# An attention and feed-forward kernel on one core: pacing of the weight decoder in the last slot of a round, order of the first score block, one load in one transfer, other PSUM banks for the first accumulators

## The chip, the core and the metric

The kernel runs on one core of a Trainium2 chip. The metric is the device time of one execution in microseconds. The kernel before took 1028.57 us in the median of three runs (1028.46 to 1028.59). Its engines are TensorE (matmuls; its weight loads are listed on their own), VectorE, ScalarE, GpSimd and SyncE, called PE, PEld, DVE, ACT, POOL and SP in the profile. SP here only issues transfers.

## What is computed

Sigmoid attention over 8 sequences of 448 positions with 12 heads of 64, then a feed-forward network on the 3584 tokens. Everything is float32.

```python
scores = scale * np.matmul(q, k.transpose(0, 1, 3, 2)) - np.log(S)   # (8, 12, 448, 448), scale 1/8
attn = 1.0 / (1.0 + np.exp(-scores))
attn_out = np.matmul(attn, v)
x = attn_out.transpose(0, 2, 1, 3).reshape(3584, 768)
h = x @ w_in                       # (768, 2048)
out = np.maximum(0.01 * h, h) @ w_out
```

## The kernel before

Float32 products are made of parts: each operand is split into a high part (a copy in the type fp32r, which TensorE multiplies fast) and a low part (the operand less its high part), and a product takes three matmuls: high by high, high by low, low by high.

**Attention** works on 48 pairs of heads (`Pair`, line 476), two pairs, x and y, in each of 24 rounds (line 794). A round has five slots: the scores of x, the scores of y, P·V of x, P·V of y, and an ending with the last keys' scores of the next pair (`last_scores`) and the last values' products (`last_v`). The keys come in blocks of 128 (c = 0, 1, 2), each with a PSUM tile of two banks, from four such tiles, which P·V uses too; the last 64 keys are handled two pairs at a time in the ending. While a round runs, the operands of the next round's pairs (z, w) are made ready: high parts on ScalarE or VectorE, low parts on VectorE, z's in slot 3 and w's in slot 4 (line 807). After P·V, ScalarE copies one half of the result to x (`half`), and after `last_v`, in the first slot of the next round, VectorE adds the other half (`keep`, line 577; `x<-x,pv` in the profile).

**Order.** Every instruction is pinned to program order on its engine. Chores for later slots are put in lists by `later`; `slot` runs the chores of its slot, then the slot's matmuls.

**Decoder.** The weights arrive as 64-bit floats. VectorE decodes them in five steps for each piece (lines 423 to 431), then adds and subtracts blocks for the fast matrix product (`firsts` for w_in, `second` for w_out), and SP stores the blocks to HBM. `prep` is a generator with one step for each `next`. In attention `prepare` (line 449) takes steps from it after each slot's work: a slot earns `PACES[n]` credits, a step costs one, and steps are taken while VectorE's counted queue is under `TIMES[n]` less 0.2. The count is kept by `counted` (line 145): 0.14 us plus columns/960 or columns/1920 for each VectorE instruction. At the end of a slot `TIMES[n]` is taken off the queue. In the feed-forward stage `fill` takes steps in a like manner.

**First feed-forward product** (`First`, line 688): seven products of a fast matrix scheme in two levels of blocks; a `Quad` of accumulators holds px, py and pz. Its PSUM pool `ps_f` has two tiles px and two tiles pz of two banks each; two unused pz tiles are taken first, so that pz has banks 0 to 3 and px banks 4 to 7. The first quad's px lay in banks 4 and 5. **Second product**: the loop over `PRODUCTS`, with operands from HBM. The change doesn't touch it.

**Start.** Pair 0's queries and keys come in four transfers, two issued by ScalarE and two by SP (`load_qk`, line 483), pair 1's in two, one on each. ScalarE then loads its sigmoid table with a small warm-up activation. `split` (line 505) makes pair 0's parts in pieces: ScalarE casts the two query halves, VectorE casts the keys and makes the low parts of keys, first and second query half, in this order. Meanwhile TensorE runs dummy matmuls into a tile `unread` (line 788). The first two score blocks are issued in halves of 224 queries (`scores`, line 516), sorted by this key (m is the part product: 0 high by high, 1 high keys by low queries, 2 low keys by high queries):

```python
todo.append((c, (m > 0 and c + 1, m, cols.start), dict(...)))
```

So both blocks' high products come first (first half of queries of block 0, then of block 1, then the second halves), then the rest of block 0, then the rest of block 1.

Of the kernel before, what the change touches and what calls it, by code (L numbers as in the profile page):

```python
# [17 lines left out]
P = 128  # L18
# [7 lines left out]
ST = 7  # L26
# [4 lines left out]
PACES = 4, 5, 4.2, 2.8, 2  # L31
TIMES = 1.92, 1.92, 2.33, 2.33, 1.66
PRODUCT, LESS, MOST = 1.8, 0.2, 4
WAIT, REST = 9, 3
FFN = 126
ALONE = 100
# [65 lines left out]
def attn_ffn_kernel(ctx: ExitStack, tc: tile.TileContext, qk, v, w_in, w_out, out):  # L102
# [240 lines left out]
    def firsts(u, dec):  # L343
        to = td[u // 2][:, :, u % 2]
        dma(out=to[:, :3], in_=dec[:, 1:])

        b12, b22, b11, b21 = (dec[:, i] for i in range(4))
        sums = block(F32, (4, HW), f"ws0_{u}")
        for place, x, y in ((2, b12, b11), (0, b22, sums[:, 2]), (1, b22, b12), (3, b21, sums[:, 0])):
            sub(sums[:, place], x, y)  # L350
            yield
        dma(out=to[:, 3:], in_=sums)

    def rest():
# [3 lines left out]
    def second(u, k, dec):  # L358


        n = len(BLOCKS)
        size = wide // 2
        e, at = u // 2, u % 2 * size
        both = {side: dec[i].rearrange("p a b -> p (a b)").rearrange("p (n m) -> p n m", n=n) for i, side in enumerate("ds")}

        def of(n, side, at, step):
            x = both[side]
            if step == 0:
                return x[:, at:at + 1].broadcast_to((P, n, size))
            end = at + (n - 1) * step + (1 if step > 0 else -1)  # L370
            return x[:, at:end if end >= 0 else None:step]

        for what, *x in PLAIN.get(k, STEPS):
            if what == "wait":
                yield from rest()
            elif what == "store":
                side, i, n, form = x
                dma(out=t2d[:, form:form + n, e, at:at + size], in_=both[side][:, i:i + n])
            else:
                n, fn, *x = x  # L380
                to, x, y = (of(n, *z) for z in x)
                if fn == "neg":
                    vec_st(out=to, in0=x, scalar=-1.0, in1=y, op0=ALU.mult, op1=ALU.subtract)
                else:
                    (add if fn == "add" else sub)(to, x, y)
                yield

    def prep():

        n = 4
        pieces = [(m, k) for m in range(len(todo)) for k in range(n)]
        raws = []

        def load():
            at = len(raws)
            if at == len(pieces):
                return
            m, k = pieces[at]  # L400
            w, u = todo[m]
            size = 4 * HW // n
            pool = (stage, "stage", 2 * HW, STAGE) if at % 2 and now < ALONE else (pp, "wr", 2 * HW, 3)
            raw = block(I32, (size, 2), f"wr{w}_{u}_{k}", pool)
            dma(out=raw.rearrange("p m t -> p (m t)"), in_=(w_in, w_out)[w][u][:, k * size:(k + 1) * size].bitcast(I32))
            raws.append(raw)

        for _ in range(3):
            load()
        yield  # L410
        for at, (m, k) in enumerate(pieces):
            w, u = todo[m]
            if k == 0 and w == 0:
                dec = block(F32, (4, HW), f"wd{w}_{u}")
            elif k == 0:
                both = [block(F32, (4, HW), f"wd{w}_{i}") for i in range(2)] if u == 0 else both[::-1]
                dec = both[0]
            raw = raws[at]
            size = 4 * HW // n
            low, high = raw[:, :, 0], raw[:, :, 1]  # L420
            tf = dec.rearrange("p b m -> p (b m)")[:, k * size:(k + 1) * size]
            t = tf.bitcast(I32)
            vec_s(out=t, in0=high, scalar1=0x7FFFFFFF, scalar2=None, op0=ALU.bitwise_and)
            yield
            vec_s(out=tf, in0=tf, scalar1=W_LEAST, scalar2=W_MOST, op0=ALU.max, op1=ALU.min)
            yield
            vec_s(out=t, in0=t, scalar1=5, scalar2=2, op0=ALU.logical_shift_left, op1=ALU.logical_shift_right)
            yield
            vec_st(out=t, in0=high, scalar=-0x40000000, in1=t, op0=ALU.bitwise_and, op1=ALU.bitwise_or)
            yield  # L430
            vec_st(out=t, in0=low, scalar=29, in1=t, op0=ALU.logical_shift_right, op1=ALU.bitwise_or)
            yield
            while len(raws) < min(at + 1 + (5 if now < ALONE else 3), len(pieces)):
                load()
            if now < ALONE:
                yield
            if w == 1:
                yield from second(u, k, both)
            elif k == n - 1:
                yield from firsts(u, dec)  # L440
            if k == n - 1:
                prepared.add((w, u))
                if w == 0:
                    yield from rest()

    preps = prep()
    credit = 0.0

    def prepare(pace, time):
        nonlocal credit, queue  # L450
        credit += pace
        while credit >= 1 and queue < time - LESS:
            next(preps, None)
            credit -= 1
        queue = max(0.0, queue - time)

# [19 lines left out]
    class Pair:  # L476
# [6 lines left out]
        def load_qk(self):  # L483
            self.raw = raws.tile([P, LAST.stop], F32, tag="qk", name=f"qk_{self.i}")
            middle, end = QUERY + S // 2, LAST.stop
            for queue, cols in {
                    0: ((dma_act, slice(QUERY, middle)), (dma, KEYS[0]), (dma_act, slice(middle, end)), (dma, slice(2 * P, QUERY))),
                    1: ((dma_act, slice(QUERY, end)), (dma, slice(0, QUERY)))}.get(self.i, ((dma, slice(0, end)),)):
                queue(out=self.raw[:, cols], in_=qk[self.i, :, cols])

        def load_v(self):
# [24 lines left out]
        def scores(self, h):  # L516
            todo, acts = [], []
            for c in range(2 * h, min(2 * h + 2, NK - 1)):
                ps = psum("s", f"sc_{self.i}_{c}")

                for cols in HALVES if self.i == h == 0 else (slice(0, S),):
                    for m, (kp, qp) in enumerate(((0, 0), (0, 1), (1, 0))):
                        for j, me in enumerate(heads):
                            todo.append((c, (m > 0 and c + 1, m, cols.start), dict(
                                out=ps[:, j, cols], lhsT=self.parts[me, kp, c * P:c * P + P],
                                rhs=self.parts[me, qp, query(cols)], start=m == 0 and cols.start == 0,
                                stop=m == 2 and cols.stop == S, skip_group_check=True)))
                acts.append((c, ps))
            if self.i == h == 0:
                todo.sort(key=lambda x: x[1])  # L530
            for n, (c, ps) in enumerate(acts):
                for x in todo if self.i == h == 0 and n == 0 else [x for x in todo if x[0] == c and (self.i or h)]:
                    mm(**x[2])
                self.a.append(self.attn(c, ps))
# [153 lines left out]
    class First:  # L688
# [6 lines left out]
        def step(self):  # L695
            t = (self.p + 1) * NU * NOP - len(self.todo)
            u, n, e = self.todo.pop(0)
            advance(t)
            p = self.p
            if n == ORDER[0] and e == 0:  # L700
                self.quad = Quad(psum, st, "st", f"h{p}_{u}", ST, leaky)
                self.c = Results()
            quad, c = self.quad, self.c
            w = w1[t // 2][1].t[:, e]
            acc, first = quad.into(n, e)
            hi, lo = self.ops.hi[n], self.ops.lo[n]
            for kk in range(NB):
                parts_mm(acc, w, slice(kk * P, kk * P + P), hi[:, kk], lo[:, kk], first and kk == 0, kk == NB - 1)
            if e == 0:
                return  # L710
            if u == NU // 2 - 1:
                self.ops.used(n)
            later(1, lambda: self.after(quad, c, u, n), first=True)
# [80 lines left out]
    for r in range(rounds):  # L794
# [15 lines left out]
        for n, work in enumerate(works):  # L810
            go([(ops[0], PLAN_ATTN.get((r, n), ""))], work)
            for t in EARLY.get((r - rounds + 1, n), ()):
                advance(t)
            prepare(PACES[n] * (r > 0), TIMES[n])

    kept, chores[now] = chores[now][0], ([], chores[now][1])
    for fn in kept:
# [4 lines left out]

    st = left.enter_context(tc.tile_pool(name="st", bufs=ST, reuse_waits="tile"))
    tiles(left, "m", "left", MORE)
    psum = banks("ps_f", dict(px=(2, 2), pz=(2, 2)))
    for n in range(2):
        psum("pz", f"first_{n}")
    size = NU * NOP

    def product(q, first, k):  # L830
# [336 lines left out]
```

## Time and profile before

| what | value |
|---|---|
| median of three runs | 1028.57 us |
| profiled execution, its own time | 1029.18 us |
| its span, first to last instruction | 1027.40 us |
| PE busy | 1023.2 us |
| PEld busy | 867.8 us |
| DVE busy | 857.2 us |
| ACT busy | 598.1 us |
| DMA | 301.1 MB, 293 GB/s in the mean |

The profile is one execution recorded by the hardware; times count from its first instruction. "Idle before" is an engine's idle time just ahead of an instruction, with what ended it, inferred from semaphores; "issue" means that nothing in the profile ended it. Where the releaser named had long been done, it was not what was waited for. The attention stage lasts to about 246 us, the first product to about 650, the second to the end.

### The profile page before, as it was taken

What the parts mean: (1) busy time and instruction counts of PE and PEld (TensorE: products, weight loads), DVE (VectorE), ACT (ScalarE), POOL (GpSimd) and SP (SyncE); (2) the same over time, 40 slices, a digit from 0 to 9 for tenths busy, and PEclk for the clock granted to TensorE, in tenths of its full rate; (3) what the DMA queues carried; (4) which work ended last, traced back from release to release, by engine and by line L of the source; (5) the groups of instructions that cost most, each with busy time, mean ns of one, the idle gap of its engine ahead of it and who ended that gap; (6) DMA issues with size and microseconds to landing.
All of it is one profiled execution on the core that took longest, in us unless ns stands there. A gap on an engine that the chain in (4) does not pass through costs nothing.

```text
span 1027.4 us, 16361 instructions
## 1 busy us (share of the span) xinstructions
PE 1023.2 (100%) x6316; PEld 867.8 (84%) x6316; DVE 857.2 (83%) x1015; ACT 598.1 (58%) x634; POOL 0.3 (0%) x5
## 2 busy tenths in 40 slices
PE   9999999999999999999999999999999999999998
PEld 6555555556999999999999999999999999999998
DVE  5889999789998899898975657699988888899883
ACT  7888888887545655555555555565362535444440
POOL 0000000000000000000000000000000000000000
PEclk9999999999999999999999999999999999999999
DMA  8888787989889898989986878997678797767833
GB/s 308 279 298 278 280 281 267 311 292 331 289 312 322 293 298 299 344 317 409 338 296 213 300 283 313 392 408 289 217 282 286 278 416 291 284 221 252 311 113 135
DMA packets 113853, 301.10 MB, mean 293 GB/s; under 512 B 9712, under 2 KB 51696, under 8 KB 113776
## 3 DMA queue, kind: packets, MB, share of 16 engines
q1 hardware_dynamic: 111760, 295.52, 80.5%
q10 hardware_dynamic: 2016, 4.54, 1.2%
q8 instruction: 50, 0.82, 0.3%
q14 instruction: 27, 0.22, 0.1%
HBM read 203.16 MB, written 96.86 MB: 292 GB/s over the span
## 4 chain that ended last, share of the span: by engine, by line
PE 99%; ACT 0%; ACTq 0%; DVE 0%; DVEq 0%; issue 0%
PE px_h L139 22%; PE acc_A L139 18%; PE acc_B L139 18%; PE pv L139 13%; PE pz_h L139 11%; PE sc L139 11%; PE py_h L139 6%; PE acc_one L139 0%; ACTq L139 0%; ACT L139 0%; DVE o L139 0%; ACT qks L139 0%; DVEq L1163 0%; ACT warm L139 0%
## 5 line engine op out<-in xcount | busy, mean ns | idle before, releaser
L139 PE MATMUL px_h<-hi,w 128*128 128x448 f32 x768 | 223.1, 361 | 0.0
L139 PEld LDWEIGHTS px_h<-hi,w 128*128 128x128 f32 x768 | 143.9, 187 | 11.3 <-ACT x L139 0.7
L139 PE MATMUL acc_A<-gh,w 128*128 128x448 f32 x528 | 151.4, 361 | 0.0
L139 DVE TENSOR_TENSOR w<-wx,w 128x768 fp32r<-128x768 f32 x112 | 106.9, 955 | 48.2 <-ACT w L139 48.2
L139 PE MATMUL px_h<-lo,w 128*128 128x448 f32 x384 | 139.4, 363 | 0.0
L139 ACT ACTIVATE s<-sc 128x896 f32<-128x896 f32 x144 | 119.4, 934 | 17.7 <-PE sc L139 17.7
L139 PE MATMUL acc_B<-gh,w 128*128 128x448 f32 x416 | 119.4, 361 | 0.0
L139 PE MATMUL pv<-s,v 64*64 64x448 f32 x1152 | 114.0, 540 | 0.0
L139 PE MATMUL pz_h<-hi,w 128*128 128x448 f32 x384 | 112.7, 361 | 0.0
L139 PEld LDWEIGHTS acc_A<-gh,w 128*128 128x128 f32 x528 | 98.9, 187 | 7.4
L139 PEld LDWEIGHTS sc<-qks 64*128 64x128 f32 x876 | 79.9, 187 | 23.6 <-issue 16.2
L139 ACT CAST w<-wx 128x768 fp32r<-128x768 f32 x112 | 92.0, 834 | 10.8 <-DMA wx<-t 10.8
L139 PE MATMUL sc<-qks 64*128 64x448 f32 (+1 forms) x876 | 95.5, 368 | 0.1
L139 PEld LDWEIGHTS pv<-s,v 64*64 64x64 f32 x1152 | 41.6, 133 | 60.9 <-issue 47.7
L139 DVE TENSOR_TENSOR w<-w 128x1536 fp32r<-128x1536 f32 x52 | 91.1, 1752 | 0.0
L139 ACT ACTIVATE c_h<-c_h 128x896 f32<-128x896 f32 x48 | 45.9, 956 | 74.1 <-DVE c_h L139 74.1
L139 PE MATMUL acc_B<-g,w 128*128 128x448 f32 x328 | 84.8, 362 | 0.0
L139 PEld LDWEIGHTS acc_B<-gh,w 128*128 128x128 f32 x416 | 77.9, 187 | 5.8
L139 ACT CAST w<-w 128x1536 fp32r<-128x1536 f32 x52 | 77.1, 1482 | 0.5 <-DMA w<-t 0.5
L139 PEld LDWEIGHTS pz_h<-hi,w 128*128 128x128 f32 x384 | 71.9, 187 | 5.3
L139 PEld LDWEIGHTS px_h<-lo,w 128*128 128x128 f32 x384 | 72.1, 188 | 3.8
L139 DVE SCALAR_TENSOR_TENSOR wd<-wr,wd 128x384 int32<-128x384 int32 x128 | 71.3, 557 | 3.2
(96 smaller groups left out, 1619.1 us busy)
## 6 DMA issues: line engine op xcount, KB each, us to landing
wx<-t SPq DMA_DIRECT2D x112, 384.0 KB, 5.4
w<-t SPq DMA_DIRECT2D x52, 768.0 KB, 4.3
g<-g SPq DMA_DIRECT2D x34, 896.0 KB, 7.4
g<-c_h SPq DMA_DIRECT2D x60, 448.0 KB, 4.4
g<-s SPq DMA_DIRECT2D x48, 448.0 KB, 5.9
qk<-in_qk SPq DMA_DIRECT2D x46, 456.0 KB, 5.2
g1s<-g SPq DMA_DIRECT2D x18, 896.0 KB, 6.1
wr<-in_w_in SPq DMA_DIRECT2D x32, 384.0 KB, 5.2
```

The lines of the kernel that those rows point to most:

```text
L139: return lambda *args, **kw: tc.keep_in_program_order(issue(*args, **kw))
```

## The change

Four parts:

1. In a round's last slot `prepare` takes a step only if the counted queue and the next step's length stay under `TIMES[n] + OVER`. Each step of the decoder now yields LONG (0.54) where the step after it is a long one, else None, which counts as SHORT (0.34).
2. The first score blocks are sorted by block; within a block high by high, then low keys by high queries, then high keys by low queries.
3. Pair 1's queries and keys come in one transfer, issued by SP in the old place; ScalarE's third transfer is gone.
4. The px tiles of the first feed-forward product have two tags, used in turn by `u`; the pool's tiles are taken in the order pz, pz, px1, px0, so that the first quad (u = 0) has banks 6 and 7.

```diff
+SHORT, LONG, OVER = 0.34, 0.54, 0.1
@@ firsts
             sub(sums[:, place], x, y)
-            yield
+            yield LONG
@@ second
-        for what, *x in PLAIN.get(k, STEPS):
+        steps = PLAIN.get(k, STEPS)
+        for m, (what, *x) in enumerate(steps):
...
-                yield
+                yield next((z[1] > 1 and LONG for z in steps[m + 1:] if z[0] == "sum"), None)
@@ prep
             vec_s(out=t, in0=t, scalar1=5, scalar2=2, op0=ALU.logical_shift_left, op1=ALU.logical_shift_right)
-            yield
+            yield LONG
             vec_st(out=t, in0=high, scalar=-0x40000000, in1=t, op0=ALU.bitwise_and, op1=ALU.bitwise_or)
-            yield
+            yield LONG
             vec_st(out=t, in0=low, scalar=29, in1=t, op0=ALU.logical_shift_right, op1=ALU.bitwise_or)
-            yield
+            yield k == n - 1 and LONG
...
             if now < ALONE:
-                yield
+                yield k == n - 1 and LONG
@@ prepare
-    credit = 0.0
+    credit, ahead = 0.0, SHORT
-    def prepare(pace, time):
-        nonlocal credit, queue
+    def prepare(pace, time, whole):
+        nonlocal credit, queue, ahead
         credit += pace
-        while credit >= 1 and queue < time - LESS:
-            next(preps, None)
+        while credit >= 1 and queue < time - LESS and (not whole or queue + ahead < time + OVER):
+            ahead = next(preps, None) or SHORT
             credit -= 1
@@ load_qk
-                    1: ((dma_act, slice(QUERY, end)), (dma, slice(0, QUERY)))}.get(self.i, ((dma, slice(0, end)),)):
+                    ...}.get(self.i, ((dma, slice(0, end)),)):
@@ scores
-                            todo.append((c, (m > 0 and c + 1, m, cols.start), dict(
+                            todo.append((c, (c, -m % 3, cols.start), dict(
...
-                                stop=m == 2 and cols.stop == S, skip_group_check=True)))
+                                stop=m == (1 if self.i == h == 0 else 2) and cols.stop == S, skip_group_check=True)))
@@ First.step
-                self.quad = Quad(psum, st, "st", f"h{p}_{u}", ST, leaky)
+                self.quad = Quad(psum, st, "st", f"h{p}_{u}", ST, leaky, (f"px{u % 2}", "pz"))
@@ the rounds
-            prepare(PACES[n] * (r > 0), TIMES[n])
+            prepare(PACES[n] * (r > 0), TIMES[n], n == len(works) - 1)
@@ after the rounds
-    psum = banks("ps_f", dict(px=(2, 2), pz=(2, 2)))
-    for n in range(2):
-        psum("pz", f"first_{n}")
+    psum = banks("ps_f", dict(pz=(2, 2), px1=(1, 2), px0=(1, 2)))
+    for x in ("pz", "pz", "px1", "px0"):
+        psum(x, f"first_{x}")
```

## Rows read from the trace of the kernel before

**Rows 1.** The page's busy times: busy us, share of the span, instructions.
```profile
PE 1023.2 (100%) x6316; PEld 867.8 (84%) x6316; DVE 857.2 (83%) x1015; ACT 598.1 (58%) x634; POOL 0.3 (0%) x5
```

**Rows 2.** The chain of waits in order of time: start us, us, what.
```profile
36.49 3.89 PE sc L139 x36
46.56 3.81 PE sc L139 x36
...
116.46 3.97 PE sc L139 x36
...
176.70 4.11 PE sc L139 x36
...
236.93 3.87 PE sc L139 x36
```

**Rows 3.** Table of waits of PE's weight loads: us in total, times, longest us.
```profile
PEld sc L139 <- DVE x L139: 1.0, 4, 0.4
```

**Rows 4.** Instructions in order of time, end of round 10: start us, us, engine, tile.
```profile
114.78 0.56 PE L139 MATMUL sc<-qk 64*64 64x448 f32 x4
...
116.61 0.55 DVE L139 TENSOR_TENSOR ws<-wd 128x384 f32<-128x384 f32 x1
117.07 1.15 DVE L139 TENSOR_TENSOR x<-x,pv 128x448 f32<-128x448 f32 x2
```

**Rows 5.** The same view, end of round 16; idle time in brackets.
```profile
173.40 1.04 DVE L139 TENSOR_TENSOR qks<-qk,qks 128x848 fp32r<-128x848 f32 x1 [0.76 <-DMA wr<-in_w_out]
...
175.02 0.56 PE L139 MATMUL sc<-qk 64*64 64x448 f32 x4
...
177.45 1.14 DVE L139 TENSOR_TENSOR x<-x,pv 128x448 f32<-128x448 f32 x2
```

**Rows 6.** The same view, ScalarE at the start.
```profile
0.73 1.37 ACTq L139 DMA_DIRECT2D qk<-in_qk  x3
2.13 1.28 ACT L139 ACT_TABLE_LOAD   x1 [2.13 <-issue]
...
4.11 0.38 ACT L139 CAST qks<-qk 128x224 fp32r<-128x224 f32 x1
```

**Rows 7.** The same view, TensorE at the start; x2 is a pair of matmuls.
```profile
4.07 0.56 PE L139 MATMUL sc<-qks 64*128 64x224 f32 x2
4.42 0.42 PE L139 MATMUL sc<-qks 64*128 64x224 f32 x2
4.63 0.68 PE L139 MATMUL sc<-qks 64*128 64x224 f32 x4
...
5.75 0.63 PE L139 MATMUL sc<-qks 64*128 64x224 f32 x4
...
6.39 0.42 PE L139 MATMUL sc<-qks 64*128 64x224 f32 x4
...
9.78 0.47 PE L139 MATMUL sc<-qks 64*128 64x448 f32 x2
```

**Rows 8.** Busy us (instructions) by engine, PEclk, DMA share, GB/s, from 4.06 to 6.44.
```profile
4.06:6.44 2.38, 2.38 (x22) 2.38 (x24) 1.25 (x5) 0.61 (x2) 0.00 (x0) 1.00 0.94 319
```

**Rows 9.** Instructions in order of time, weight loads of P·V, start and round 1.
```profile
7.36 0.21 PEld L139 LDWEIGHTS pv<-s,v 64*64 64x64 f32 x8 [0.31 <-ACT s L139]
...
20.26 0.21 PEld L139 LDWEIGHTS pv<-s,v 64*64 64x64 f32 x8 [0.30 <-ACT s L139]
```

**Rows 10.** Transfers issued in the first microseconds: queue, KB each, us to landing.
```profile
qk<-in_qk ACTq DMA_DIRECT2D x1, 256.0 KB, 5.1
...
qk<-in_qk ACTq DMA_DIRECT2D x1, 144.0 KB, 2.9
qk<-in_qk SPq DMA_DIRECT2D x1, 128.0 KB, 2.7
```

**Rows 11.** Instructions in order of time, handovers to scores and to the first product.
```profile
16.46 0.19 PEld L139 LDWEIGHTS sc<-qks 64*128 64x128 f32 x2 [0.70 <-PE sc L139]
...
246.15 0.19 PEld L139 LDWEIGHTS px_h<-hi,w 128*128 128x128 f32 x1 [0.71 <-ACT x L139]
...
247.10 1.15 DVE L139 TENSOR_TENSOR x<-x,pv 128x448 f32<-128x448 f32 x2
```

## What the change will do: the prediction

> **What bounds the kernel now.** I read the page's busy times first: TensorE is busy 1023.2 us, all but some 4 us of the span [rows 1], so only what stretches its own chain can move the time. Next I read the chain of waits in order of time. It is TensorE from the first scores to the end, and in both feed-forward stages its pieces repeat to the hundredth, so the parts of this change can win nothing there. In the attention stage the 36 score matmuls at a round's start take 3.81 us in 17 of 23 rounds and longer in six: 3.89, 3.97 twice, 4.11, 3.83 and 3.87 [rows 2]. These are 0.08, 0.16, 0.16, 0.30, 0.02 and 0.06 us too many, 0.78 in all. The table of waits names the cause of most: weight loads of the scores waited for VectorE's addition into x four times, 1.0 us in sum [rows 3]. The rest of what may be had is the start: before its first score pair TensorE does only dummy products.
>
> **Part one: the last slot of a round.** The addition into x (`keep`) frees a PSUM tile that the next round's scores need. VectorE works in order: in the last slot it does the low part of pair w, then what `prepare` gives it, then both additions. I measure from the slot's first matmul to the start of the additions. End of round 10: 114.78 to 117.07, 2.29 us, loss 0.16; here a decoding step of 0.55 us stands between the low part and the additions [rows 4]. End of round 16: 175.02 to 177.45, 2.43 us, loss 0.30 [rows 5]. Both give the loss as the offset less 2.13 us, and a long step in this slot is what crosses that line.
>
> The new condition lets a step in only if queue + ahead < time + 0.1, that is below 1.76. I followed the counts slot by slot; they are constants (0.14 us + columns/960, or /1920 for the one-input form). With 1.02 for the low part and a remainder of 0 to 0.31 from the slot before, a long step (0.54) fits only where the remainder is under 0.20. The ends of rounds 10 and 12 (now a step at 1.34, up to 1.88), 16 (1.28 to 1.82), 18 and 22 lose that step; 16 gets a short one instead (1.25 to 1.59), 18 none, 22 keeps its first step only. The expected gain is 0.16 + 0.16 + 0.30 + 0.02 + 0.06 = 0.70 us. The 0.08 us of the round at 36.49 stay: no step of length stands in the slot before it.
>
> One remainder is priced. In round 16 VectorE was late before the slot began: pair z's low part, one slot earlier, started at 173.40 after 0.76 us idle on a transfer of raw weights [rows 5]. A short step in place of the long one moves the additions from 2.43 to 2.23 us (0.54 less 0.34 by the counts), which leaves 0.10 us; whether that transfer is late again I cannot say, so I take half, 0.05. Part one: -0.65 us, bounds -0.70 and -0.20 (the latter if the lateness mostly moves to other rounds).
>
> What is put off goes to the first slots of the next round, behind the additions, under the unchanged limit. By the same counts the decoder is at most one slot later through the w_in blocks, level again at the first w_out block, and two steps behind at the first feed-forward product, at most 1.1 us of VectorE. `fill` takes them up in a stage where the chain shows no stretched piece. If that cover were gone, the weights' low parts would be late by these 1.1 us; they are made two products ahead. The transfers that those steps issue on SP go out with them; behind them in SP's queue stand loads for several slots later. Cost taken: nothing.
>
> **Part two: the first block.** Now the first halves of both blocks come first (pairs at 4.07 and 4.42), then the second halves, which need ScalarE's second cast (start 4.11 [rows 6]) and run at 4.63 [rows 7]. After the change the pair that waits is second in line, and the other block's pair, which filled the time at 4.42, stands behind five more. TensorE then idles until about 4.63 and has one pair of 224 columns more to do afterwards. Does anything gain by block 0 being ready earlier? It would be complete one place sooner, and its sigmoid too, but P·V at 7.36 does not wait for the sigmoid: its weight load sat idle 0.31 us behind the scores, and in a steady round, where that sigmoid is long done, 0.30 [rows 9]; the releaser named in both is only the last one by the profile. So the start is TensorE's own chain from 4.63 on, and one more pair costs what a pair costs at the rate of the rounds: 3.81/18 = 0.21 us for 448 columns, 0.11 for 224. Part two: +0.11 us. Upper bound +0.32: the pair at the early rate, 0.21 us (two pairs in 0.63 at 5.75, one alone 0.42 [rows 7]), and another 0.11. Lower bound -0.20: see part three. I take +0.11, since both waits are read from their own rows.
>
> **Part three: pair 1 in one transfer.** ScalarE issues three transfers in 1.37 us and then loads its table, 1.28 us from 2.13 [rows 6]; without the third the table load ends some 0.46 us earlier (a third of 1.37). That shortens nothing if the casts wait for data. The second query half (144 KB), issued at about 1.17, landed 2.9 us later, near 4.07 [rows 10], and its cast began at 4.11: the landing decides. Pair 1's packets stand behind it in the same queue. If the halves nevertheless landed as fast as SP's 128 KB of that moment (2.7 us [rows 10]), the start would be 0.20 us sooner: the lower bound. Pair 1's larger part, issued at about 1.65, took 5.1 us and was there near 6.7 [rows 10], three microseconds before its scores at 9.78 [rows 7]; SP issues the whole at its old place, and only pair 1's high and low parts lie between. Taken: 0.
>
> **Part four: banks.** The first accumulators move from banks 4 and 5 (last pair's third score block) to 6 and 7 (its second); P·V itself needs the sigmoids that empty both. The weight load of the first product idles 0.71 us, that of a steady round's first score 0.70 [rows 11]: the handover has no wait in it, so 0. If that is wrong, a tile in the banks of the last P·V would wait from 246.15 for additions that run 1.15 us from 247.10 [rows 11], 2.1 us; those are banks 0 to 3, so I leave it out.
>
> **Sum.** -0.65 + 0.11 + 0 + 0 = -0.54 us. The profiled execution took 1029.18 us, its span 1027.40 and 1.78 around it; that becomes 1028.64. It was 0.61 above the median of the runs, 1028.57, so the prediction is 1028.57 - 0.54 = 1028.03, rounded 1028.0.
>
> **Rivals.** (a) The start gains instead: casts 0.20 us earlier and the new order free of its gap, 1028.57 - 0.65 - 0.20 = 1027.7. For it: 0.46 us come off ScalarE's queue. Against: the landing near 4.07. (b) The gate doesn't do what it says: the counts miss waits for transfers, like the 0.76 us above, so additions stay late in other rounds, 1028.57 - 0.20 + 0.11 = 1028.5, at most 1028.8. (c) Slower, by TensorE's clock. The stretch from 4.06 to 6.44 us prints a granted clock of 1.00 [rows 8], yet its pairs are 0.21 us apart for 224 columns, and the rounds' pairs 0.21 us for 448: the lower level, 1.2 GHz, then 2.4, with the step near 6.4 us (two pairs in 0.42 from 6.39 [rows 7]). Before the rise the engine worked almost without a break, dummies and then scores. The change puts a gap of some 0.2 us there, between the first and the second pair. If the rise came later for it, every microsecond of work at the higher level would cost one more: half of the 3.3 us between that step and the end of pair 0's P·V (9.78) gives 1028.0 + 1.7 = 1029.7, all of it 1031.3. It decides as soon as that gap counts as idleness. The Trainium skill ("TensorE: Matmul & The Clock Gate", Part 1) has it that the engine starts throttled and that its activity releases the clock, which speaks against a new gap in this place; the trace has only the one rise, with no such gap before it, so no run here shows it.
>
> **How the numbers follow.** Forecast 0.63 (its own range 1027.8 to 1028.4), (a) 0.15, (b) 0.17, (c) 0.05. From 1027.5 to 1028.8 the forecast, (a) and (b) are held with their bounds; (c) is left out. A difference of 0.2%, 2.06 us, is about what a measurement of this kernel can tell from no change. Faster by more, below 1026.5: no case reaches it, 0.02 for what I don't see. Slower by more, above 1030.6: the heavier part of (c), and part four's 2.1 us with another loss, 0.04. Within: 0.94.
>
> **What the profile after would show.** Right: the score pieces of the chain at the starts of rounds 11, 13 and 17 at 3.81 us (17 perhaps to 3.91), no or one wait of the score weight loads for the addition into x; the second score pair near 4.63 with a gap before it and P·V at about 7.47; 0.7 us idle before the first product. Wrong: the second cast well before 4.11, P·V before 7.36, pairs of 224 columns still 0.21 us apart past 6.5 us, or score pieces over 3.81 in rounds that had none.

## The result and the profile after

The changed kernel takes 1040.31 us in the median of six runs (1036.46 to 1041.63); beside it the kernel before took 1028.58. The ratio is 1.0103, with a 95% interval from 1.0090 to 1.0115: 1.0% slower, where 1028.0 was forecast. The profiled execution took 1041.63 us. (One execution of all that are told of here, the first of the gate alone, took 2092.29 us, with TensorE busy for 2086.2 of them, and enters no figure.) The page of the profiled execution, span and busy times:

```profile
span 1039.8 us, 16357 instructions
...
PE 1027.9 (99%) x6316; PEld 870.8 (84%) x6316; DVE 857.3 (82%) x1015; ACT 597.8 (57%) x634; POOL 0.3 (0%) x5
```

Beside [rows 1] TensorE is busy 4.7 us longer for the same 6316 matmuls, and the span is 12.4 us longer. So TensorE waits some 7.7 us, and some of its work runs slower. Both traces hold all 6316 matmuls, from the 46th on in the same order, so the start of each can be compared with that of its counterpart. The difference (after less before) grows in five places:

| where | difference | step |
|---|---|---|
| scores and P·V of pair 0, to 10.4 us | 0 to 1.81 | +1.81 (0.19 of it stands at 6.4 us) |
| attention, rounds 2 to 24 | 1.81 to 2.60 | +0.79 (won 0.08, 0.16, 0.16, 0.30, 0.06; lost 0.58 near 170 us, 0.97 near 191) |
| first product, one place, 642.08 us | 2.60 to 3.53 | +0.93 |
| third product of the second stage, its first matmul, 673.57 us | 3.53 to 9.70 | +6.17 |
| the matmuls after that one | 9.70 to 12.37 | +2.67 |

The table of waits, TensorE's matmuls (us in total, times, longest), names three of the five:

```profile
PE acc_A L140 <- ACT o L140: 6.0, 1, 6.0
PE sc L140 <- DVE x L140: 1.0, 2, 0.7
...
PE px_h L140 <- ACT c_h L140: 0.6, 1, 0.6
```

In the kernel before this table has no wait but TensorE's own start. The chain of waits in order of time (start, us, what) says what stands behind them:

```profile
118.19 3.81 PE sc L140 x36
...
138.17 3.81 PE sc L140 x36
...
161.50 3.59 DMA t<-wd
...
169.17 0.63 DVE x L140
...
190.20 0.54 DVE x L140
...
248.83 3.80 PE px_h L140 x18
...
657.39 12.38 DMA g<-s
...
671.04 2.48 ACT o L140 x2
...
673.57 10.03 PE acc_A L140 x36
683.60 7.20 PE acc_B L140 x36
```

The same piece of acc_A in the kernel before:

```profile
664.03 7.20 PE acc_A L139 x36
```

Three things are to be seen. The pieces at 118.19 and 138.17, the starts of rounds 11 and 13, are 3.81 us where they were 3.97 each [rows 2]: the gate does what it was forecast to do. But at 161.50 the chain leaves TensorE. A store of a decoded block (`t<-wd`) takes 3.59 us from issue to landing, VectorE has work for the first 2 us of that and idles for the rest, and the additions into x come late after all:

```profile
165.21 0.37 DVE L140 TENSOR_SCALAR wd<-wr 128x384 int32<-128x384 int32 x1 [1.74 <-DMA t<-wd]
```

And the largest wait is in a stage where the prediction expected no change: ScalarE's copies of the first output tiles (`o`) wait for a store of a sum (`g<-s`) that ScalarE itself issued at 657.39 and that took 12.38 us. ScalarE in order of time, after and then before:

```profile
669.87 3.64 ACT L140 COPY o<-acc_A 128x1344 f32<-128x1344 f32 x3 [8.63 <-DMA g<-s]
```
```profile
657.46 3.63 ACT L139 COPY o<-acc_A 128x1344 f32<-128x1344 f32 x3
```

Before, the same three copies run without any idle time ahead of them. The store itself is hardly slower than it was. The last store of a sum from issue to landing (KB, us), before and then after:

```profile
g<-s ACTq DMA_DIRECT2D x1, 448.0 KB, 11.9
```
```profile
g<-s ACTq DMA_DIRECT2D x1, 448.0 KB, 12.4
```

So what is new is not a late store but that something waits for it.

The remaining steps, the +2.67 and all but 0.19 of the +1.81, are TensorE's clock. (The 0.19 is the gap itself and stands before the kernel before gets its higher clock: the third score pair starts at 4.87 us where it started at 4.63.) The table by stretches (busy us and instructions by engine, then granted clock, DMA share, GB/s), after:

```profile
6.44:10.10 3.66, 3.66 (x26) 2.06 (x28) 1.34 (x2) 2.28 (x3) 0.00 (x0) 1.00 1.00 389
...
673.50:679.10 5.60, 5.53 (x15) 4.93 (x16) 3.97 (x3) 5.53 (x5) 0.00 (x0) 0.50 1.01 424
679.10:685.00 5.90, 5.90 (x31) 5.53 (x30) 4.69 (x3) 3.07 (x2) 0.00 (x0) 1.00 1.01 392
```

The first of these stretches before:

```profile
6.44:10.10 3.66, 3.66 (x40) 1.68 (x40) 1.64 (x2) 2.49 (x4) 0.00 (x0) 1.00 1.01 384
```

Right behind the 6-us wait the granted clock is 0.50, the lower level of 1.2 GHz, and 15 matmuls take 5.53 us where the next stretch does 31 in 5.90. The mean granted clock of the whole execution is 0.995 to 0.997 in all six runs of the changed kernel, and 0.999 or 1.000 in every execution of the kernel before beside the experiments. At the start TensorE does 26 matmuls in the time of 40. The printed 1.00 misleads there, as in [rows 8]; the records of the granted clock begin with the rise to full rate, at 6.44 us before and at 10.10 after.

### The profile page after: what moved, and what is told of

Same layout as the page of the kernel before. It is cut to its first block, busy times and chain, and to the rows that moved or that the text cites. A ratio compares the mean times of both kernels' runs of the same rounds, so it can differ in the third digit from the quotient of the medians.

```text
span 1039.8 us, 16357 instructions
## 1 busy us (share of the span) xinstructions
PE 1027.9 (99%) x6316; PEld 870.8 (84%) x6316; DVE 857.3 (82%) x1015; ACT 597.8 (57%) x634; POOL 0.3 (0%) x5
## 4 chain that ended last, share of the span: by engine, by line
PE 93%; DMA 3%; DVE 1%; ACT 1%; issue 1%; SPq 0%; DVEq 0%; ACTq 0%
PE px_h L140 21%; PE acc_A L140 18%; PE acc_B L140 17%; PE pv L140 11%; PE pz_h L140 10%; PE sc L140 10%; PE py_h L140 5%; DMA g<-s 1%; DMA wx<-t 1%; DMA g<-c_h 1%; PE acc_one L140 0%; DVE wd L140 0%; DVE qks L140 0%; DMA t<-wd 0%; PE unread L140 0%
## 5 line engine op out<-in xcount | busy, mean ns | idle before, releaser
L140 PE MATMUL acc_A<-gh,w 128*128 128x448 f32 x528 | 154.7, 367 | 6.0 <-ACT o L140 6.0
L140 PEld LDWEIGHTS px_h<-hi,w 128*128 128x128 f32 x768 | 143.9, 187 | 12.4 <-ACT c_h L140 1.0
```

The source lines that it names most:

```text
L140: return lambda *args, **kw: tc.keep_in_program_order(issue(*args, **kw))
```

## The experiments

Sizes of the parts first (each part alone, and all but one), then the causes.

**The gate alone.** Part one of the change on the kernel before, nothing else:

```diff
-        while credit >= 1 and queue < time - LESS:
-            next(preps, None)
+        while credit >= 1 and queue < time - LESS and (not whole or queue + ahead < time + OVER):
+            ahead = next(preps, None) or SHORT
...
```

> The kernel before with the gate in the last slot alone (order, transfers and banks as before). Theory 'buffer': the gate puts decoding steps off, this shifts the order in which the seven buffers of the sums (st) are reused, and the last sum that ScalarE stores lands in a buffer under the first output tile of the second product; ScalarE's first copy into that tile waits for this store. Then the gate alone gives the 6.0 us wait of acc_A for ScalarE's o and the fall of the clock behind it (about +8.9 us in the second product), the +0.9 in the first product and the two stalls of +0.6 and +1.0 in attention, less 0.8 won at the starts of rounds: about 1039.1, and no late rise of the clock at the start. Rival 'traffic': the store was late because one transfer fewer moved the other transfers; then the gate alone leaves the second product as it was: between 1027.8 and 1029.5.

Measured: 1037.49 to 1041.58 us in four executions, ratio 1.0105 (1.0091 to 1.0119). For a profile the same kernel was run once more:

> The gate alone, once more for its profile. Theory 'buffer': TensorE's acc_A waits about 5 to 6 us for ScalarE's o near 667 us, ScalarE's copy waits for the store of s (7 to 9 us), the granted clock falls to 0.5 behind it, and matmuls run at the lower rate for some microseconds: some 1037.5 to 1041.5. Attention as in the run with the output tiles moved: +0.9 us in all. Rival: no such wait without the other parts, 1029.9.

Measured: 1037.98 and 1036.87 us, ratio 1.0084 (1.0065 to 1.0102). Table of waits from 650 to 690 us, and the chain:

```profile
ACT o L140 <- DMA g<-s: 8.5, 1, 8.5
...
PE acc_A L140 <- ACT o L140: 5.9, 1, 5.9
```
```profile
654.35 12.34 DMA g<-s
...
670.49 9.39 PE acc_A L140 x36
```

The wait is the gate's, with the other three parts absent. The differences to the kernel before, by matmul, are +0.86 in attention from round 2 on (won 0.67, lost 0.62 and 0.92), +6.07 for the wait and +2.03 for the clock behind it. 'Traffic' falls.

**The order alone.**

```diff
-                            todo.append((c, (m > 0 and c + 1, m, cols.start), dict(
+                            todo.append((c, (c, -m % 3, cols.start), dict(
...
```

> The kernel before with the new order of the first blocks alone. Theory 'clock': the gap between the first and the second score pair puts off the rise of the granted clock from 6.44 to about 10.1 us, and round 1 begins about 1.8 us later, everything behind it as before: 1030.4. Rival 'early start': the later rise belongs to ScalarE's missing transfer, which lets the first pair start at 3.92 in place of 4.07; then the order alone costs 0.1 us: 1028.7.

Measured: 1028.79 us, ratio 1.0002 (0.9993 to 1.0011). In this profile the clock rises at 3.72 us, ahead of the gap. So neither theory holds as it stood: the order does not put the rise off in each execution. But 2 of 11 executions took 1030.66 and 1030.92; all others lie between 1028.27 and 1029.08. The kernel before has such executions too, though fewer: of the 75 taken beside the experiments one took 1030.30 and one 1030.86, and no profile shows why.

**The transfer alone.**

```diff
-                    1: ((dma_act, slice(QUERY, end)), (dma, slice(0, QUERY)))}.get(self.i, ((dma, slice(0, end)),)):
+                    }.get(self.i, ((dma, slice(0, end)),)):
```

> The kernel before with pair 1 in one transfer, alone. In this kernel the last pair's P.V comes to lie in PSUM banks 4 and 5 (2 and 3 in the kernel before), where the first px of the first product lies too. Theory 'handover': that px waits for the additions into x of the last pair, and the table of waits shows TensorE waiting for VectorE's x at about 246 us: up to +2.1 us, 1030.7. Rival: other work covers it, as the prediction had it for the banks: 1028.6, with 0.7 us idle before the first product. For the start: a clock that rises at 6.44 says that the missing transfer alone does not put it off.

Measured: 1032.08 us, ratio 1.0034 (1.0022 to 1.0047): slower by itself. Up to the first product its matmuls stand within 0.2 us of the kernel before. There the chain and the stretch behind it read:

```profile
247.06 1.07 DVE x L139 x2
...
248.18 5.45 PE px_h L139 x18
```
```profile
248.95:252.30 3.35, 3.35 (x11) 2.95 (x10) 3.31 (x6) 0.00 (x0) 0.00 (x0) 0.50 1.01 366
252.40:256.00 3.60, 3.60 (x20) 3.38 (x19) 0.39 (x2) 2.33 (x3) 0.00 (x0) 1.00 0.86 267
```

The table of waits has it as one wait:

```profile
PE px_h L139 <- DVE x L139: 2.1, 1, 2.1
```

TensorE waits 2.1 us for VectorE's additions into x, and in this profile the clock falls behind the wait: the piece of the first product that takes 3.80 us in the changed kernel (at 248.83 in its chain) takes 5.45 here. It doesn't fall each time. Two of the five executions, this one (1032.85) and the one of 1033.34, have a mean granted clock of 0.998; the other three (1031.30, 1031.83, 1032.08) have 0.999 or 1.000, like the kernel before, so there the clock did not fall for long, if at all. By the programs' addresses the last pair's P·V lies in banks 2 and 3 in the kernel before, and in 4 and 5 wherever the transfer is merged: one transfer less is enough to turn round which free PSUM tile each score block gets. (The two more dummy products of the run with the gap filled, below, do the same.)

**All but the order.** Parts one, three and four together.

> The changed kernel with the old order of the first blocks. Theory 'clock': only the 1.8 us of the start come back, the clock rises near 6.4 us: 1040.3 - 1.8 = 1038.5. Rival 'early start': the start stays as in the changed kernel and the time too, 1040.3 (or 0.1 less). The wait of acc_A for o at about 667 us stays in both.

Measured: 1040.11 us, ratio 1.0111 (1.0096 to 1.0127), as the changed kernel. In its profile the clock rises at 4.20 us; TensorE's wait for o is there (5.3 us), and no wait at 246 us: the new banks take away what the merged transfer brings. Of the 11.7 us that the change costs, the order makes no part that can be seen in a median; the executions of all kernels with the wait for o spread over 5 us (1036.46 to 1041.63), so a part of 1 or 2 us could hide there.

**The first output tiles elsewhere.** By the programs' addresses the first output tile of the second product lies over the fifth and sixth of the seven places in which the first product's results and sums were kept. In the kernel before, these two places last hold results whose stores go out ahead of the sums'. With the gate (and a rest of nine steps, below) they hold two of the last sums, one of them the last that is stored at all. In the programs of the order alone and of the transfer alone they hold what they hold in the kernel before, so it is the gate that changes this. This edit, on the gate alone, takes five unused tiles ahead of the first output tile, so that none of the first three lies there:

```diff
     outp = ctx.enter_context(tc.tile_pool(name="outp", bufs=OO, reuse_waits="tile"))
+    for x in range(5):
+        nc.gpsimd.memset(outp.tile([P, NC // 2, S], F32, tag="out", name=f"first_{x}")[:, 0, :1], 0.0)
```

> The gate alone, and the first output tiles of the second product in other buffers: five unused tiles, each with one column set to zero by GpSimd, are taken ahead of them, so that none of the three tiles that the first product fills lies over a buffer of the sums (st). Theory 'buffer': the wait of acc_A for ScalarE's o (5.3 and 6.0 us in the traces so far) and the fall of the clock behind it are gone; what is left of the gate is -0.5 to -0.7 at the starts of rounds and its two stalls in attention (0.6 and 0.9): 1028.87 + 0.1 to + 1.7, that is 1029.0 to 1030.5. Rival 'traffic': ScalarE or TensorE waits for something else that the store only accompanies; then the wait stays and so does the time, 1039.7.

Measured: 1029.91 us, ratio 1.0012 (1.0003 to 1.0021). The gate alone had a median of 1039.64 in the four executions of its first run and 1037.43 in the two of its second, so this is some 7.5 to 9.7 us less. The table of waits and the chain:

```profile
POOL first L1024 <- DMA g<-s: 667.3, 1, 667.3
...
ACT o L140 <- POOL first L1024: 1.0, 1, 1.0
```
```profile
657.40 7.20 PE acc_B L140 x36
664.60 7.20 PE acc_A L140 x36
```

The store is still there, but GpSimd waits for it now (from the start of the program, hence the 667.3), and ScalarE for 1.0 us, for a later tile; and TensorE's pieces are 7.20 us without a stretch. 'Buffer' is shown. The same edit on the whole change:

> The changed kernel, whole, with the first output tiles moved in the same way. Theory 'buffer': some 9 us less than the changed kernel: 1029.5 to 1031.5, with now and then a run 2 us longer, where the clock rises late at the start. Rival: within 1 us of the changed kernel's 1040.3.

Measured: 1029.73 us, ratio 1.0013 (1.0004 to 1.0022), with 1031.71 and 1033.73 among 11 runs. This profile has another small cost, at the start. VectorE, then TensorE's waits:

```profile
8.42 0.60 DVE L140 CAST qks<-qk 128x848 fp32r<-128x848 f32 x1 [3.19 <-DMA qk<-in_qk]
```
```profile
PE sc L140 <- DVE qks L140: 0.8, 2, 0.5
```

The cast of pair 1's operands waits for the merged transfer. It began at 8.42 us here and at 8.72 in the changed kernel, at 6.80 and 7.00 in the two others that have this transfer, and at 6.99 in the kernel before. Where the clock rises early, at 3.92 us in this profile, TensorE gets to pair 1's scores before their parts are made. Whether this cost or a late rise of the clock makes the two long executions isn't shown.

**The stalls in attention.** With the gate, VectorE in order of time shows the first decoding step of a block late, in the run with the output tiles moved:

```profile
163.31 0.38 DVE L140 TENSOR_SCALAR wd<-wr 128x384 int32<-128x384 int32 x1 [1.76 <-DMA t<-wd]
...
183.52 0.36 DVE L140 TENSOR_SCALAR wd<-wr 128x384 int32<-128x384 int32 x1 [1.53 <-issue]
```

The kernel before has 0.46 us of idle time at the first of these places, for the same store. At the second place the profile names no releaser, but the store of that block was issued at 180.02 us and landed 3.4 us later, just ahead of the step:

```profile
t<-wd SPq DMA_DIRECT2D x1, 576.0 KB, 3.4
```

After each w_in block the decoder rests nine steps (`WAIT`) so that the block's store can land before the next block overwrites its buffer. My reading is that the gate puts a step off and the next slots make it up, so that the nine steps pass in less time; no run counts them. A longer rest should help:

```diff
-WAIT, REST = 9, 3
+WAIT, REST = 12, 3
```

> As the run with the gate alone and the first output tiles moved, and the decoder's rest after each w_in block is 12 steps in place of 9. Theory: the two stalls in attention (at about 163 to 168 and 183 to 189 us) are VectorE's wait for the store of the block before, whose buffer the next block's first step overwrites; steps put off by the gate are made up quickly, so that this first step comes sooner behind the store than in the kernel before, where it idled 0.46 and 0.45. Three more steps of rest, each worth about 0.55 us (18 steps in a round of 10 us), take 1.65 us off these idle times of 1.76 and 1.80: the stalls go, and the time is 1028.87 - 0.7 = 1028.2 (1027.9 to 1028.5). Rival: the stalls come from the queue behind them on VectorE, whatever the rest; then 1029.0 to 1030.5 as without it.

> The gate alone, first output tiles moved, and a rest of 10 steps. The rest of 12 took the stalls of attention away (0.5 us better than 9) but left more for the first product, where TensorE waited 0.65 us for a low part of the weights at 257.7 us. One step more than 9 takes 0.55 us off VectorE's idle times of 1.76 and 1.53 us: the stalls shrink from 0.6 and 0.9 to about 0.1 and 0.4, and the first product keeps its cover: 1029.0. Rival: the wait at 257.7 us comes from the gate's put-off steps alone, then it shows here too: 1029.6.

> The same with a rest of 11 steps: 1.1 us off idle times of 1.76 and 1.53. Theory: no stall in attention, the gain of the gate (0.5 to 0.7 us) shows: 1028.2 to 1028.5, if the first product has no wait at 257.7; with that wait (0.65) 1028.9 to 1029.1.

Measured: 1029.43 us with 12 (ratio 1.0005, 0.9996 to 1.0014), 1030.87 with 10 (1.0018, 1.0009 to 1.0027), 1029.19 with 11 (1.0003, 0.9994 to 1.0012). With 11 and 12 the stalls are gone, and with 11 the gate's gain stands in the trace at last: 0.16, 0.16 and 0.30 us at rounds 11, 13 and 17 and 0.06 at the last, 0.68 in all. (The last 0.06 can't be put down to the gate: the order alone shows 0.04 there and the transfer alone 0.06.) But the put-off steps, more of them now, reach the first product, where a low part of the weights is late at 257 us. TensorE's waits with a rest of 12:

```profile
PE pz_h L140 <- DVE w L140: 0.6, 1, 0.6
```

By the difference of the matmuls this place costs 0.85 us with 12, 0.53 with 11 and 0.78 with 10. And with 10 the stall isn't smaller but has moved to another block, as VectorE's row shows:

```profile
123.47 0.36 DVE L140 TENSOR_SCALAR wd<-wr 128x384 int32<-128x384 int32 x1 [2.36 <-DMA t<-wd]
```

TensorE's wait for it is 1.30 us, at 128.45 us, and the granted clock behind it stays at 1.00:

```profile
PE sc L140 <- DVE x L140: 1.3, 1, 1.3
```
```profile
128.00:135.00 7.00, 6.55 (x68) 3.87 (x72) 6.83 (x13) 5.83 (x8) 0.00 (x0) 1.00 0.74 268
```

That the stall moves was not expected. The store explains each of these stalls, but which block meets it follows from the whole sequence of steps, not from the length of the rest alone.

**The late rise of the clock.** Two more dummy products in the gap that the new order leaves, on order and banks:

```diff
+                    if self.i == h == n == 0 and at == 2:
+                        for _ in range(2):
+                            mm(unread[heads[0], :S // 4], lhsT=zeros[:, :D], rhs=zeros, start=True, stop=True)
                     mm(**x[2])
...
```

> The kernel before with the new order of the first blocks, two more dummy products of 112 columns between the first and the second score pair, where the new order leaves a gap, and the new banks (without them the first px would share banks with the last P.V in this kernel). Theory 'restart': the clock rises some 3.4 us later in an execution where the gap falls badly (2 of 11 runs of the order alone were at 1030.7 and 1030.9, the others at 1028.3 to 1029.1); with the gap filled no run is later than 1029.6, and the median is 1028.9 to 1029.1, by up to 0.2 us of dummies too many. Rival: these runs have another cause; then some are again 2 us longer.

Measured: 1029.37 us, ratio 1.0010 (1.0001 to 1.0018), and 5 of 11 runs at 1030.98 to 1031.56. The weight loads at the start:

```profile
3.96 0.29 PEld L139 LDWEIGHTS sc<-qks 64*128 64x128 f32 x2 [0.32 <-ACT qks L139]
4.45 0.66 PEld L139 LDWEIGHTS unread<-const-float32-0.0 128*64 128x64 f32 x4 [0.20 <-issue]
5.38 3.22 PEld L139 LDWEIGHTS sc<-qks 64*128 64x128 f32 x28 [0.28 <-issue]
```

By the records the matmuls now follow one another without idle time (the second pair begins at 5.38, which is later than the 4.42 of the order alone), and still this profile's clock rises at 9.94 us. 'Restart' by a gap falls. The last run keeps the gap out in another way, with both blocks' first halves ahead as in the kernel before and only then block 0, block 1:

```diff
-                            todo.append((c, (c, -m % 3, cols.start), dict(
+                            todo.append((c, (m + cols.start > 0 and c + 1, -m % 3, cols.start), dict(
...
```

> The kernel before with the first halves of both blocks first, as in the kernel before, and then the rest of block 0, then the rest of block 1; and the new banks. So the pair that waits for ScalarE's second cast is third, not second. Theory 'early pair': what makes some runs 2 us longer (clock risen at 9.94 and 10.10 us in two profiles of the new order, at 3.7 to 6.7 in all others) is that TensorE has only one score pair to do until the second cast is through; with two pairs before it all runs are at 1028.3 to 1029.6, median 1028.8. Rival 'block order': it is the order of what follows, weights and blocks taken in another sequence; then 2 to 5 of 11 runs are at 1030.5 or above, as with the new order.

Measured: 1028.78 us, ratio 0.9998 (0.9990 to 1.0007), all 11 runs between 1028.30 and 1029.06. So the order of the rest looks harmless, and what seems to count is that TensorE has one pair of scores, not two, until the second cast is through. That is likely and not shown: with a share of long executions as in the order alone (2 of 11), 11 good ones in a row would come up by chance once in nine times, and the kernel before has two long ones of 75. The rises in all profiles:

| first score pairs | rise of the granted clock, us |
|---|---|
| two before the second cast | 3.72, 4.20, 4.37, 5.61, 5.92, 6.44, 6.56, 6.57, 6.73 |
| one before it (the new order) | 3.72, 3.92, 9.94, 10.10 |

The rise moves by 3 us among profiles of kernels with two pairs ahead of the second cast. The Trainium skill ("TensorE: Matmul & The Clock Gate", Part 1) has it that the same kernel rises at different points of its run; these rows agree, though each is another kernel's. With the new order the rise comes at about 10 us in two of four profiles, and the one of them that has no other cost (the gap filled) took 1031.56, some 2 us more than its kernel's shorter executions. Why score pairs seem to keep it early and dummy products in their place don't was not tried further and stays open.

## Why the prediction was wrong

**The step that failed is the last paragraph of part one: "Cost taken: nothing" for what is put off.** I followed the put-off steps by their number and their time on VectorE, 1.1 us, and asked only whether work two products ahead covers them. Three things were missing there.

First, a step that moves also moves when a buffer comes free, and here the buffers of the sums are given out in the order in which they come free. The put-off steps changed this order in the last sums of the first product. The output tiles of the next stage lie over them, and by this the last store, 12.4 us from issue to landing, got a reader that waits. Cost: 6.2 us in the changed kernel, 6.1 in the gate alone, 5.4 with all parts but the order, and with the tiles moved nothing. The store was not the new thing (11.9 us in the kernel before); its reader was.

Second, a wait of TensorE costs more than itself. The clock falls behind it, which adds 2.7 us in the changed kernel, 2.0 in the gate alone and 1.8 with all parts but the order. All 16 executions of the kernels with this wait (three of them profiled) show it in their mean clock, 0.995 to 0.997. Behind the 2.1 us of the merged transfer it adds 1.6 in the profile, but falls in two of five executions only, and the waits in attention, of up to 0.7 us and once 1.30, show no such fall. I had told of this clock for the start alone, in rival (c).

Third, the steps' own store. I wrote that the transfers "go out with them", and looked at what stands behind them on SP; but the next block's first step waits for the landing of that store, and the slot limit does not count such a wait. Attention lost 1.55 us in two stalls in the changed kernel against 0.76 won there. Of rival (b), "the counts miss waits for transfers", this is the mechanism, with 1.55 us three times as dear as the 0.45 that it would take away from the gain.

**The opening was wrong in what it left out.** "In both feed-forward stages its pieces repeat to the hundredth, so the parts of this change can win nothing there" is true, but a stage in which nothing waits has all the more to lose, and 9.8 of the 12.4 us came there.

**What of part one was right.** The loss is the additions' offset less 2.13 us, and keeping the long step out wins it: 0.62 us seen with a rest of 11 at the three rounds that are surely the gate's, 0.68 with the last, against the 0.65 forecast, and the start of round 17 got all of its 0.30. That the whole sum agrees so well is in part luck: the 0.05 held back for round 17 was not needed, and the 0.06 of the last round went without the gate too. (The 0.08 us of the round at 36.49, which I let stay, went in the changed kernel; they go with the merged transfer alone too.) A version with this gain and none of the costs would be 0.07% faster, less than the half-width of the intervals here (about 0.09%); none of the kernels run was faster than the kernel before beyond the noise.

**Part two.** The forecast +0.11 lies inside the measured interval (1.0002, 0.9993 to 1.0011), which is some 0.9 us wide on each side and so confirms little. Rival (c) was put at 0.05 and is what the changed kernel's profile shows: 1.6 us of slower clock behind a gap of 0.2, where 1.7 to 3.3 were worked out. By the times it occurs in some executions only (2 of 11 with the order alone, 5 with the gap filled), and the gap that I named isn't what it takes, since the late rise comes with the gap filled too.

**Part three.** Nothing at the start, as forecast, in the transfer alone, where the matmuls of pair 0 end within 0.02 us of the kernel before; in one profile with an early rise TensorE waited 0.8 us, because the merged transfer can land 1.4 to 1.7 us later than the two did (casts at 8.42 and 8.72 against 6.99). The claim that "only pair 1's high and low parts lie between" held; that a merged transfer would change anything 240 us later was not considered.

**Part four.** The mechanism was seen and its size right: 2.1 us priced, 2.12 measured in the transfer alone, with 1.6 more for the clock in its profile. The failed step is "those are banks 0 to 3, so I leave it out". I read the banks from the kernel before; in the changed one the last P·V lies in 4 and 5, and the new banks are what keeps this loss away. Part four isn't a change without effect: without it the merged transfer costs 3.2 us.

**What is left over.** The 0.93 us at 642 us stands in the changed kernel's profile alone, where ScalarE's queue issued a result store late, by the chain behind a load of weights (`wx<-t`, 10.91 us). None of the other profiles with the gate shows it; it wasn't followed further. Nor was the spread of 5 us among the executions with the wait for o: the three profiles read account for 1036.68, 1037.98 and 1041.63, and a lower mean clock (0.995 where others have 0.997) goes with some of the long ones, not with all.

## What to carry to other kernels

Where buffers are given out in the order in which they come free, any edit of the order of work re-deals them, far from the edit as well: before an edit is priced at nothing, compare the two programs' addresses and banks, and look for a late store under the first tiles of the next stage. Price a wait of the bounding engine with the slower clock that may follow it, not alone. And where a rest is counted in steps, work that is made up faster shortens it in time.

## What the runs showed of the hardware

A wait of 2.1 us can be enough to lower TensorE's clock: behind it 11 matmuls took 3.35 us at a granted clock of 0.50, then 20 took 3.60 at 1.00. The Trainium skill ("TensorE: Matmul & The Clock Gate", Part 1) says that activity releases the clock; these rows agree. But the same wait left the mean clock at 0.999 or 1.000 in three of five executions. Waits of 5.3 to 6.0 us lowered it in all three profiles that have one, and the 13 other executions of these kernels have the same mean clock of 0.995 to 0.997. Waits of 0.7 and 1.30 us in attention left it at full rate.

A store of a sum of 448 KB that ScalarE issued behind three like it took 11.9 us to land in the kernel before, 12.4 in the changed kernel and 12.3 in the gate alone, where the first of the four took 4.5 in the kernel before. And one transfer of 456 KB in place of two of 256 and 200 KB was followed by its cast as early as these in two profiles, and 1.4 and 1.7 us later in two others.
